# Two of four gate blocks with a second level of Winograd's scheme, in the last two groups of an attention and FFN kernel

## The chip, the cores and the metric

The kernel runs on one core of a Trainium2 chip. A core has five engines that run their own instruction streams and wait for each other by semaphores: TensorE (PE, matmuls out of SBUF into PSUM, with weight loads shown apart as PEld), VectorE (DVE), ScalarE (ACT), GpSimd (POOL) and SyncE (SP, which here only issues DMAs). The metric is the device time of one execution in microseconds, as the median of several runs.

## The reference

A linear attention whose normed output is the input of a multiplicative feed-forward network. All arrays are f32.

```python
batch, n_heads, seq, head_dim = (8, 8, 576, 64)
kv  = np.einsum('bhsd,bhse->bhde', k, v)
out = np.einsum('bhsd,bhde->bhse', q, kv)
rms = np.sqrt(np.mean(out * out, axis=-1, keepdims=True) + 1e-06)
attn_out = out / rms * g_norm
x = attn_out.transpose(0, 2, 1, 3).reshape(4608, 512)
# w1, w2: (512, 1024)   w3: (1024, 1024)   w_out: (1024, 512)
a = x @ w1
b = x @ w2
h = a * b @ w3
return h @ w_out
```

## The kernel before, in words

**Groups.** The 4608 tokens are worked in nine groups of 512: for each of the eight batches its first 512 tokens, and one group of the eight times 64 tokens that are left (called group 8, its input is `x_left`). The order is 0 to 6, then 8, then 7 (`groups`, L824). `w3 @ w_out` is folded into one matrix `w3o` at the start, so a group has two parts: the gates, ab = (x @ w1) * (x @ w2), and the output, ab @ w3o. The attention of the next batch is cut into pieces that are woven into the gates of the current group (`steps`, L518, called by `between`); groups 8 and 7 have none left to weave in.

**Winograd's scheme.** Every product of matrices is cut into 2 x 2 blocks and made with 7 block products in place of 8, with sums of blocks ahead (s1 to s4 of one side, t1 to t4 of the other) and behind. `winograd` (L610) is one such level: it keeps the products p1, p5, u2 and u3 by a ScalarE copy from PSUM (`keep`, L628), lets other products add up onto the same bank, and calls `done` for each of the four output blocks c12, c22, c11, c21, in that order.

**Gates.** `gates(T, p, between, ready)` (L742) makes a quarter of the gates of group T: p runs over the NF = 4 blocks. A product is 4 matmuls of 128 x 128 weights with 256 columns of x (two halves, for w1 and w2, and two chunks), so a block has 28. VectorE adds the two parts of an output block and multiplies its w1 half by its w2 half into `ab[i][:, p, j, :]` (L756, L757; for c21 L752, L753). Then `sum_ab(p)` makes the four sums of the block that the output needs (VectorE, 128x256). In the last block (p = 3) these sums, and the first of the inner ones, are given to `gates` as `ready` actions, and VectorE's order is from there on the written one (`in_order`, L1130). TensorE, GpSimd and SP are in the written order throughout; ScalarE is ordered by the scheduler.

**Output.** `project_twice(T, last, ahead)` (L864) uses two levels: 7 outer products of 7 inner products of 2 matmuls with 128 columns each, 98 matmuls. An outer product fills two PSUM banks, with 4 and 3 of its inner products (`products`, L877); `keep` (L908) copies both to SBUF on ScalarE, `add` (L937) adds a product from PSUM on VectorE, and `finish` (L914) makes an output block of the 7 inner products with four VectorE additions (L920 to L923). The inner sums of the ab side are made by `sum_inner` (L849) just ahead, into three sets of small tiles `inner_sums`, with the last one in place. The w3o side with all its sums is prepared once, in group 1 (`prepare_b`, L795), kept in DRAM (`w3o_l2`, 896 KB for each of the 7 parts), and streamed back for every group through three places in SBUF (`streams`) and the done group's x (`load_b`, L827; each load waits until the matmuls that read the place before are done). At the end of a group's output stage `load_b` has begun the first three parts of the next group's. `ahead` holds the four subtractions that make t1 to t4 of the next group's x (`combine_x`, L717).

**Pools.** `late_tile` gives the tiles p1, p5 and u (u2, u3 and u4 share one); PSUM has five banks named mm and three named at. `tick` (L542) is a one-column GpSimd copy whose only use is to wait for a late tile.

Of the kernel before, what the change touches and what calls it, by code (L numbers as in the profile page):

```python
# [2 lines left out]

# [8 lines left out]
FP32 = mybir.dt.float32  # L12
# [9 lines left out]
def kernel(  # L22
# [32 lines left out]
    nc = tc.nc  # L55
    PSUM = bass.MemoryType.PSUM
    P = 128

    B, H, S, D = q.shape
    DM = H * D  # L60
    DF = w1.shape[1]
    NP = H // 2
    KF = DF // P
    NH = KF // 2
    J = 4
    G = J * P
    N = G // 2
# [5 lines left out]
    inp = ctx.enter_context(tc.tile_pool(name="inp", bufs=2))  # L73
    work = ctx.enter_context(tc.tile_pool(name="work", bufs=2))
    ps_mm = ctx.enter_context(tc.tile_pool(name="ps_mm", bufs=5, space=PSUM))
    ps_at = ctx.enter_context(tc.tile_pool(name="ps_at", bufs=3, space=PSUM))
# [5 lines left out]
    def bank(pool, tag):  # L82
        return pool.tile([P, 512], FP32, name=tag, tag=tag)
# [31 lines left out]
    NF = KF // 2  # L115
# [488 lines left out]
    late = {}  # L604
    tick = const.tile([P, 1], FP32, name="tick")

    def late_tile(name):
        return late_pool.tile([P, 7, P], FP32, name=name[0] if name[0] == "u" else name)
# [65 lines left out]
    def run(*step_lists):  # L674

        for steps in zip(*step_lists):
            for step in steps:
                step()
# [38 lines left out]
    def combine_x(T):  # L717
        xb[T] = {f"b{i + 1}{j + 1}": xT[T][:, i, j] for i in range(2) for j in range(2)}
        return combine(xb[T], parts(xc))
# [9 lines left out]
    def sum_ab(p):  # L729
        aa[p] = {f"a{i + 1}{j + 1}": ab[j][:, p, i, :] for i in range(2) for j in range(2)}  # L730
        return sums(aa[p], free["ab", p])
# [10 lines left out]
    def gates(T, p, between, ready=lambda name: None):  # L742
        def done(name, one, two):
            multiply(name, one, two)
            ready(name)

        def multiply(name, one, two):

            dst = ab[int(name[1]) - 1][:, p, int(name[2]) - 1, :]
            if two is None:  # L750
                c = late_pool.tile([P, N], FP32, name="c21")
                nc.scalar.copy(c, one[:, 0, :])  # L752
                nc.vector.tensor_mul(dst, c, one[:, 1, :])  # L753
                return
            c = late_pool.tile([P, 2, N], FP32, name="c")
            nc.vector.tensor_add(c, one, two)  # L756
            nc.vector.tensor_mul(dst, c[:, 0, :], c[:, 1, :])  # L757

        winograd(
            lambda name, w, c: wa[p][name][:, w, c, :],  # L760
            lambda name, c: xb[T][name][:, c, :],
            NP // 2, done, between,
        )


    def project(T, between):
        def done(name, one, two):
            half, j = int(name[1]) - 1, int(name[2]) - 1
            dst = o_sbs[half][:, :, j * N:(j + 1) * N]
            if two is None:  # L770
                nc.scalar.copy(dst, one)
            else:
                nc.vector.tensor_add(dst, one, two)
            if name in ("c11", "c21"):
                rows = out[T * S:T * S + G, :].rearrange("(p j) f -> p j f", j=J)
                nc.sync.dma_start(out=rows[:, 2 * half:2 * half + 2, :], in_=o_sbs[half])

        winograd(
            lambda name, m, p: aa[p][name][:, m * P:(m + 1) * P],
            lambda name, p: ob[p][name],  # L780
            NF, done, between,
        )
# [12 lines left out]
    def prepare_b():  # L795

        nc.sync.dma_start(
            out=w3o_l2[7, :, 0:1024].rearrange("p (f n) -> p f n", n=N), in_=b_blocks()[5]
        )
        for n, y in enumerate(b_blocks()):  # L800
            b11, b12, b21, b22 = (
                y[:, 2 * i:2 * i + 2, j * P:(j + 1) * P] for i in range(2) for j in range(2)
            )


            stage = w3o_sums[0].rearrange("p f n -> p (f n)") if n == 4 else (
                o_sbs[(n - n // 5) % 2].rearrange("p m n -> p (m n)")
            )
            stage = stage[:, 0:6 * P]
            t1, t2, t4 = (t.rearrange("p (c n) -> p c n", n=P) for t in (  # L810
                stage[:, i * 2 * P:(i + 1) * 2 * P] for i in range(3)
            ))
            nc.vector.tensor_sub(t1, b12, b11)
            nc.vector.tensor_sub(t2, b22, t1)
            nc.vector.tensor_sub(b12, b22, b12)
            nc.vector.tensor_sub(t4, b21, t2)
            nc.sync.dma_start(
                out=w3o_l2[n, :, 0:1024].rearrange("p (f n) -> p f n", n=N), in_=y
            )
            nc.sync.dma_start(out=w3o_l2[n, :, 1024:PART], in_=stage)  # L820
            yield
# [5 lines left out]
    def load_b():  # L827
        n = len(loaded_b)
        if n == ALL_B:
            return  # L830
        i = n % 7
        t = streams[n % 3] if n < 7 else streams[(i + 1 if i < 3 else i) % 3]
        if n >= 7 and i == 3:
            done_with = xT[groups[1 + n // 7]]
            t = done_with.rearrange("p i j r n -> p (i j r n)")[:, 0:PART]

        part = {ALL_B - 2: 6, ALL_B - 1: 7}.get(n, n % 7)

        queue = nc.scalar if i in ((3, 5) if n < 7 else (4, 6)) else nc.sync
        if n + 1 < ALL_B:  # L840
            queue.dma_start(out=t, in_=w3o_l2[part])
        else:
            t = t[:, 0:1024]
            queue.dma_start(out=t, in_=w3o_l2[part, :, 0:1024])
        loaded_b.append(t)
# [15 lines left out]
        nc.vector.tensor_sub(a21, a11, a21)  # L861
        inner[n] = [a11, a12, a22, s1, s2, s4, a21]

    def project_twice(T, last, ahead):  # L864
        def store(half):
            if T < B:
                rows = out[T * S:T * S + G, :].rearrange("(p j) f -> p j f", j=J)
# [121 lines left out]

            add(p5, r1)  # L990
        z = keep("u3", r1)
        load_b()
        if not last:
            sum_inner(6)
            nc.vector.tensor_add(p5, p5, z)
        finish(p5, 1, 1)
        products(6 if last else 5, r2)
        load_b()
        if last:
            add(z, r2)  # L1000
            finish(z, 1, 0)
            last_block()
        else:
            add(p1, r2)
            finish(p1, 0, 0)
            products(6, r1)
            load_b()
            finish(keep("u4", r1), 1, 0)

    done = {}  # L1010
    dram = ctx.enter_context(tc.tile_pool(name="dram", bufs=1, space=bass.MemoryType.DRAM))
    w3o_l2 = dram.tile([8, P, PART], FP32, name="w3o_l2")


    ctx.enter_context(tc.manual_schedule(
# [92 lines left out]
    for n, T in enumerate(groups):  # L1108
        pieces = steps(T + 1) if n + 2 < NG else iter([])

        def between():
            next(pieces, lambda: None)()
            if T == 1:
                for _ in range(2):
                    if next(preparing, 0) == 0 and len(loaded_b) < 3:
                        load_b()

        for p in range(NF):
            if T and p + 1 == NF:
                sum_1, sum_2, sum_4, sum_3 = sum_ab(p)  # L1120
                following = {
                    "c12": [], "c22": [sum_1],
                    "c11": [
                        lambda: sum_inner(0, lambda: all_of(f() for f in (sum_2, sum_3))),
                        lambda: sum_inner(1),
                    ],
                    "c21": [sum_4],
                }

                in_order = tc.manual_schedule(engines={mybir.EngineType.DVE})  # L1130
                in_order.__enter__()
                gates(T, p, between, lambda name: all_of(f() for f in following[name]))
                continue
            gates(T, p, between if T or p else lambda: None)
            if T == 0:
                if p + 1 < NF:
                    run(sum_w(p + 1))
                for n in range(2):
                    if len(converted) < len(todo):
                        ahead = [copies["xT"] if p == 0 else copies["u3"][0], copies["u2"][p]][n]  # L1140
                        with tc.issue_after(ahead.ins):
                            begin_next()
                        end_next()
                if p + 1 == NF:
                    allocate_projection()
                    run(*(f(i) for i in range(NF) for f in (sum_ab, combine_w3o)))
            else:
                run(sum_ab(p))
        last = n + 1 == NG
        if T:  # L1150
            project_twice(T, last, [] if last else combine_x(groups[n + 1]))
            in_order.__exit__(None, None, None)
            continue
        project(T, between)
        run(combine_x(1))
        preparing = prepare_b()
        third = late_pool.tile([P, 3, 2, P], FP32, name="inner_sums")
        inner_sums.append([third[:, i] for i in range(3)])

# [29 lines left out]
```

## Time and profile before

| | us |
|---|---|
| median of 4 runs (767.14 to 769.38) | 767.76 |
| the profiled execution | 767.95 |
| its span | 766.2 |
| gates of group 8, four blocks (621.92 to 670.27 in the span) | 48.35 |
| output of group 8 (670.27 to 692.16) | 21.89 |
| gates of group 7, four blocks (692.16 to 740.51) | 48.35 |
| output of group 7 and the last stores (740.51 to 766.2) | 25.7 |

The span is the time between the first and the last instruction of the profiled execution; the 1.75 us that its time has more lie around it. Group 8 and group 7 have the same stages, one after the other. The granted TensorE clock is 1.00 in every stage listed.

How such lines are read: a timeline line has the start in us from the span's beginning, the length, the engine, the source line, the operation, what it writes and reads with the program's names (buffer numbers left out), shapes, a count when several alike are merged, and in brackets how long the engine stood idle before it and whose end released it. A line of a group table has, after the count, the busy time in us, the mean of one instruction in ns, and the idle time before. Program names in the trace are those of the place in SBUF: "raw" stands for the sums of ab and for the output tiles, "w3o_sb" for two of the three stream places.

### The profile page before, as it was taken

What the parts mean: (1) busy time and instruction counts of PE and PEld (TensorE: products, weight loads), DVE (VectorE), ACT (ScalarE), POOL (GpSimd) and SP (SyncE); (2) the same over time, 40 slices, a digit from 0 to 9 for tenths busy, and PEclk for the clock granted to TensorE, in tenths of its full rate; (3) what the DMA queues carried; (4) which work ended last, traced back from release to release, by engine and by line L of the source; (5) the groups of instructions that cost most, each with busy time, mean ns of one, the idle gap of its engine ahead of it and who ended that gap; (6) DMA issues with size and microseconds to landing.
All of it is one profiled execution on the core that took longest, in us unless ns stands there. A gap on an engine that the chain in (4) does not pass through costs nothing.

```text
span 766.2 us, 14419 instructions
## 1 busy us (share of the span) xinstructions
PE 758.0 (99%) x5775; PEld 659.4 (86%) x5775; DVE 543.3 (71%) x1083; ACT 253.2 (33%) x479; POOL 135.7 (18%) x132
## 2 busy tenths in 40 slices
PE   7999999999999999999999999999999999999998
PEld 5455788888899889988998899889988998898897
DVE  6977999548878468846775687667755864495467
ACT  6776764213222332233222322232133222222221
POOL 0000000223510441043114411331144000000000
PEclk9999999999999999999999999999999999999999
DMA  9997641338997836773568466835652560065024
GB/s 319 334 336 198 200 137 44 83 84 255 323 304 263 236 99 165 228 209 108 170 218 211 113 182 219 203 103 177 231 103 49 182 210 1 7 228 159 1 79 148
DMA packets 133159, 132.55 MB, mean 173 GB/s; under 512 B 76644, under 2 KB 121188, under 8 KB 133092
## 3 DMA queue, kind: packets, MB, share of 16 engines
q1 hardware_dynamic: 130640, 117.20, 52.3%
q10 hardware_dynamic: 2452, 14.42, 5.6%
q8 instruction: 46, 0.75, 0.4%
q14 instruction: 21, 0.17, 0.1%
HBM read 100.27 MB, written 16.38 MB: 152 GB/s over the span
## 4 chain that ended last, share of the span: by engine, by line
PE 97%; DMA 2%; ACT 0%; issue 0%; SPq 0%; DVE 0%; ACTq 0%
PE mm L617 60%; PE mm L899 23%; PE mm L596 7%; PE at L332 3%; PE at L415 2%; DMA raw<-in_moe_w_out_dram 1%; PE at L583 1%; PE at L351 1%; PE at L950 0%; DMA raw<-in_moe_w_dram 0%; PE at L449 0%; PE at L434 0%; ACT ab L157 0%; ACT kv_sb L343 0%; ACT chunks L158 0%; PE mm L434 0%
## 5 line engine op out<-in xcount | busy, mean ns | idle before, releaser
L617 PE MATMUL mm<-xT,w_sb 128*128 128x256 f32 x768 | 176.2, 379 | 0.0
L617 PEld LDWEIGHTS mm<-xT,w_sb 128*128 128x128 f32 x768 | 145.5, 190 | 20.0 <-issue 0.5
L617 PE MATMUL mm<-xc,ws 128*128 128x256 f32 x576 | 130.2, 379 | 0.0
L617 PEld LDWEIGHTS mm<-xc,ws 128*128 128x128 f32 x576 | 109.3, 190 | 15.0 <-ACT p L630 0.2
L756 DVE TENSOR_TENSOR c<-mm,u 128x512 f32<-128x512 f32 x36 | 24.9, 690 | 102.8 <-PE mm L617 102.8
L630 ACT COPY u<-mm 128x512 f32<-128x512 f32 x74 | 43.4, 587 | 137.8 <-PE mm L617 127.8
L630 ACT COPY p<-mm 128x512 f32<-128x512 f32 x74 | 43.4, 586 | 88.0 <-PE mm L617 84.7
L617 PE MATMUL mm<-xc,w_sb 128*128 128x256 f32 x288 | 69.0, 382 | 0.0
L596 PE MATMUL mm<-chunks,ab 128*128 128x512 f32 x128 | 60.3, 603 | 2.5 <-DVE chunks L170 1.7
L290 POOL COPY xT<-xn 128x1024 uint16<-128x1024 uint16 x26 | 31.2, 1227 | 177.7 <-DVE xn L393 177.7
L617 PE MATMUL mm<-xT,ws 128*128 128x256 f32 x256 | 61.1, 381 | 0.0
L617 PEld LDWEIGHTS mm<-xc,w_sb 128*128 128x128 f32 x288 | 53.9, 190 | 7.7 <-ACT u L630 0.3
L757 DVE TENSOR_TENSOR ab<-c 128x256 f32<-128x256 f32 x108 | 57.9, 536 | 3.0
L617 PEld LDWEIGHTS mm<-xT,ws 128*128 128x128 f32 x256 | 48.0, 190 | 6.6
L384 DVE TENSOR_REDUCE inv<-sq 128x8 f32<-128x512 f32 (+1 forms) x40 | 23.4, 627 | 39.3 <-ACT sq L383 39.3
L899 PE MATMUL mm<-w3o_sb,raw 128*128 128x128 f32 x372 | 48.6, 276 | 0.1
L899 PE MATMUL mm<-w3o_sb,ab 128*128 128x128 f32 x368 | 48.6, 275 | 0.0
L756 DVE TENSOR_TENSOR c<-p,u 128x512 f32<-128x512 f32 x36 | 27.1, 752 | 27.4 <-ACT u L630 27.4
L899 PEld LDWEIGHTS mm<-w3o_sb,ab 128*128 128x128 f32 x368 | 45.4, 192 | 0.4
L899 PEld LDWEIGHTS mm<-w3o_sb,raw 128*128 128x128 f32 x372 | 44.9, 192 | 0.5 <-DVE raw L857 0.2
L596 PEld LDWEIGHTS mm<-chunks,ab 128*128 128x128 f32 x128 | 21.8, 190 | 25.1 <-issue 15.8
L910 ACT COPY u<-mm 128x512 f32<-128x512 f32 x23 | 13.5, 586 | 85.7 <-DVE raw L923 63.3
(166 smaller groups left out, 1169.0 us busy)
## 6 DMA issues: line engine op xcount, KB each, us to landing
w3o_sb<-w3o_l SPq DMA_DIRECT2D x18, 896.0 KB, 6.1
raw<-in_moe_w_dram SPq DMA_DIRECT2D x31, 512.0 KB, 7.4
raw<-w3o_l SPq DMA_DIRECT2D x15, 896.0 KB, 4.7
w3o_sb<-w3o_l ACTq DMA_DIRECT2D x14, 896.0 KB, 4.5
k_sb<-in_k_dram SPq DMA_DIRECT2D x32, 256.0 KB, 3.8
v_sb<-in_v_dram SPq DMA_DIRECT2D x32, 256.0 KB, 4.7
q_sb<-in_q_dram SPq DMA_DIRECT2D x32, 256.0 KB, 4.2
out_dram<-raw SPq DMA_DIRECT2D x14, 512.0 KB, 3.5
```

The source lines that it names most:

```text
L290: nc.gpsimd.tensor_copy(to, src.rearrange("p a n w -> p w a n"))
L332: nc.tensor.matmul(kv_ps[e * D:(e + 1) * D, r - rs[0], :], lhsT=k_sb[:, e, cols] if j < J else kl[:, 2 * r + e, :], rhs=v_sb[:, e, cols] i ...
L351: nc.tensor.transpose(qt_ps[:, e, i, :], q_sb[:, e, i * P:(i + 1) * P], ident)
L384: nc.vector.tensor_reduce(out=inv[:, i], in_=sq.rearrange("p (h d) -> p h d", d=D), axis=AX.X, op=ALU.add)
L415: nc.tensor.matmul(o_ps[l][tokens, n * D:(n + 1) * D], lhsT=qT[r][rows, e, i, tokens], rhs=kv_b[rows, e, r, :], start=True, stop=True,)
L596: nc.tensor.matmul(sums_ps[half][m], lhsT=w3T[half, c][:, m, :], rhs=chunks[:, c, 1, :], start=(c == 0), stop=(c == KF - 1),)
L617: nc.tensor.matmul(ps[:, u, :], lhsT=lhsT(a_name, u, c), rhs=rhs(b_name, c),  start=(u == 0 and c == 0 and to is None), stop=(c == chunks ...
L630: copies.setdefault(name, []).append(nc.scalar.copy(t, ps))
L756: nc.vector.tensor_add(c, one, two)
L757: nc.vector.tensor_mul(dst, c[:, 0, :], c[:, 1, :])
L899: nc.tensor.matmul(to[:, i, :], lhsT=x[:, c, :], rhs=y[:, c, :], start=new and place // 4 not in seen, stop=(c == 1), skip_group_check=True,)
L910: nc.scalar.copy(t[:, 0:4], ps[0])
```

## The change

In groups 8 and 7 (`TWICE`) the gates are made in the order: block 2 as before, then blocks 0 and 1 together with a second level, then block 3 as before.

- `gates_of_two(T)` runs the 7 outer products in two column halves (w = 0 for w1, w = 1 for w2). Each outer product is again cut in 2 x 2: the weights by the two blocks (m) and the two chunks (c), x by its two chunks and the two halves of its 256 tokens. So an outer product is 7 matmuls of 128 columns in two PSUM banks, 49 for a half and 98 for the two halves. The order of the outer products is written so that the output block c11 comes first (after two products); its second product goes to two of the at banks. Product 5 and product 6 of a half both go to the banks of `r1`. The copies of u3 and u4 go to places of their own (`places`, in the tile names xT and xn), the rest to p1, p5 and u as before. Each half makes its four output blocks with `finish`; the second half writes to a tile c and multiplies it into the first half's result.
- The inner sums of the weights (s1, s2, s4 of each of the 7 outer blocks, 128x256 each) are made once on VectorE in groups 3 and 4 by `prepare_w`, one of its seven steps in each call of `between` in blocks 0 and 1, and stored to DRAM (`w_l2`) from SP. The fourth sum is made in place in group 6, block 2 (`replace_a21`). They come back in three loads of 896 KB (`load_w`), issued at the end of the output stage ahead of group 8 and of group 7 where `load_b` was called; the three `load_b` calls stand in `gates_of_two` instead, in its second half.
- The inner sums of x (4 for each of the 7 outer blocks, 28 of 128x128) are made by GpSimd in block 2 (`sum_x`), behind a `tick` on p1, into the places of k, v, q and qT tiles, which have no other use by then.
- The four sums of ab for blocks 0 and 1 are made by GpSimd with four instructions for both blocks (`sum_ab_two`), behind `gates_of_two`, in place of `sum_ab(0)` and `sum_ab(1)` on VectorE.
- VectorE's written order begins at `gates_of_two` in these groups.

```diff
+    def w_blocks(name):
+        return [wa[m][name][:, :, c, :] for m in range(2) for c in range(2)]
+
+    def prepare_w():
+        for n, (name, _) in enumerate(PRODUCTS):
+            a11, a12, a21, a22 = w_blocks(name)
+            s1, s2, s4 = inner_sums[2 * (n % 2)]
+            nc.vector.tensor_add(s1, a21, a22)
+            nc.vector.tensor_sub(s2, s1, a11)
+            nc.vector.tensor_sub(s4, a12, s2)
+            for i, s in enumerate((s1, s2, s4)):
+                at = (3 * n + i) * 2 * P
+                nc.sync.dma_start(
+                    out=w_l2[:, at:at + 2 * P].rearrange("p (w m) -> p w m", w=2), in_=s
+                )
+            yield
+
+    def replace_a21():
+        for name, _ in PRODUCTS:
+            a11, _, a21, _ = w_blocks(name)
+            nc.vector.tensor_sub(a21, a11, a21)
...
+    def load_w():
+        n = len(loaded_w)
+        t = streams[(n + 1) % len(streams)]
+        nc.sync.dma_start(out=t, in_=w_l2[:, n * PART:(n + 1) * PART])
+        loaded_w.append(t)
...
+    def sum_x(T):
...
+        nc.gpsimd.tensor_copy(tick, late["p1"][:, 0, 0:1])
+        for t, (_, name) in zip(x_sums, PRODUCTS):
+            b11, b12, b21, b22 = (
+                xb[T][name][:, c, i * P:(i + 1) * P] for c in range(2) for i in range(2)
+            )
+            t1, t2, t3, t4 = t
+            nc.gpsimd.tensor_sub(t1, b12, b11)
+            nc.gpsimd.tensor_sub(t2, b22, t1)
+            nc.gpsimd.tensor_sub(t3, b22, b12)
+            nc.gpsimd.tensor_sub(t4, b21, t2)
...
+    def gates_of_two(T):
...
+        def products(n, w, ps, new):
...
+            for place, x, y in (
+                (0, a11, b11), (3, a12, b21), (1, a22, t4), (2, s1, t1), (6, s2, t2), (5, s4, b22),
+                (4, s3, t3),
+            ):
+                nc.tensor.matmul(
+                    ps[place // 4][:, place % 4, :], lhsT=x, rhs=y,
+                    start=new and place // 4 not in seen, stop=True, skip_group_check=True,
+                )
+                seen.add(place // 4)
+            if w == 1 and n in (2, 4, 6):
+                load_b()
+            return ps
...
+        def finish(z, w, i, j):
...
+            dst = ab[i][:, 0:2, j, :].rearrange("p m (n t) -> p m n t", t=P)
+            to = dst
+            if w:
+                to = late_pool.tile([P, 2, N], FP32, name="c").rearrange("p m (n t) -> p m n t", t=P)
+            nc.vector.tensor_add(z[:, 6], z[:, 6], z[:, 0])
+            nc.vector.tensor_add(z[:, 4:6], z[:, 4:6], wide(6))
+            nc.vector.tensor_add(to[:, 1], z[:, 1:3], wide(4))
+            nc.vector.tensor_add(to[:, 0], z[:, 3:6:2], z[:, 0:3:2])
+            if w:
+                nc.vector.tensor_mul(dst, dst, to)
+
+        for w in range(2):
+            r1 = products(0, w, banks(ps_mm, "mm"), True)
+            p1 = keep(late_tile("p1"), r1)
+            r3 = products(1, w, banks(ps_at, "at"), True)
+            add(p1, r3)
+            finish(p1, w, 0, 0)
+            r2 = products(2, w, banks(ps_mm, "mm"), True)
+            p5 = keep(places[2] if w else late_tile("p5"), r2)
+            products(3, w, r1, False)
+            z = keep(late_tile("u2"), r1)
+            products(4, w, r2, False)
+            add(z, r2)
+            finish(z, w, 0, 1)
+            products(5, w, r1, False)
+            u3 = keep(places[0], r1)
+            nc.vector.tensor_add(p5, p5, u3)
+            finish(p5, w, 1, 1)
+            products(6, w, r1, False)
+            finish(keep(places[1], r1), w, 1, 0)
+        loaded_w.clear()
+
+    def sum_ab_two():
+        c11, c12, c21, c22 = (ab[i][:, 0:2, j, :] for i in range(2) for j in range(2))
+        s1, s2, s4 = (t[:, 0:2] for t in ab_sums)
+        nc.gpsimd.tensor_add(s1, c12, c22)
+        nc.gpsimd.tensor_sub(s2, s1, c11)
+        nc.gpsimd.tensor_sub(c12, c11, c12)
+        nc.gpsimd.tensor_sub(s4, c21, s2)
...
+    PRODUCTS = [
+        ("a11", "b11"), ("a12", "b21"), ("s1", "t1"), ("s2", "t2"), ("s4", "b22"), ("s3", "t3"),
+        ("a22", "t4"),
+    ]
+    TWICE = (B, B - 1)
...
+            if T in (3, 4) and p < 2:
+                next(preparing_w, 0)
+            if T == B - 2 and p == 2 and not replaced:
+                replaced.append(True)
+                replace_a21()
+
+        if T in TWICE:
+            once = iter([T])
+            gates(T, 2, lambda: [sum_x(t) for t in islice(once, 1)])
+            run(sum_ab(2))
+            in_order = tc.manual_schedule(engines={mybir.EngineType.DVE})
+            in_order.__enter__()
+            gates_of_two(T)
+            sum_ab_two()
         for p in range(NF):
+            if T in TWICE and p + 1 < NF:
+                continue
...
-            project_twice(T, last, [] if last else combine_x(groups[n + 1]))
+            project_twice(
+                T, last, [] if last else combine_x(groups[n + 1]),
+                load_w if not last and groups[n + 1] in TWICE else load_b,
+            )
```

In `project_twice` the three `load_b()` calls behind products 4, 5 and 6 become `load_after()`, its new argument.

## The prediction

> **What bounds the kernel.** I read the engine totals and the chain that ended last first, then the timeline of TensorE over the last two groups, then tables by stage of that stretch, and last the timelines of VectorE, ScalarE and GpSimd there.
>
> ```profile
> PE 758.0 (99%) x5775; PEld 659.4 (86%) x5775; DVE 543.3 (71%) x1083; ACT 253.2 (33%) x479; POOL 135.7 (18%) x132
> PE 97%; DMA 2%; ACT 0%; issue 0%; SPq 0%; DVE 0%; ACTq 0%
> ```
>
> TensorE is busy 99% and holds 97% of the chain: only fewer or cheaper matmuls, or new gaps between them, can move the time. The stage table of group 8 (columns: stretch, its length, busy us and instructions of PE, PEld, DVE, ACT, POOL, granted clock, DMA share, GB/s), four gate blocks and the output stage:
>
> ```profile
> 621.92:634.01 12.09, 12.09 (x58) 10.65 (x57) 6.46 (x15) 2.82 (x5) 0.00 (x0) 1.00 0.59 193
> 634.01:646.10 12.09, 12.09 (x57) 10.64 (x56) 5.21 (x12) 2.72 (x5) 0.00 (x0) 1.00 0.00 0
> 646.10:658.19 12.09, 12.09 (x58) 10.64 (x57) 5.21 (x12) 2.72 (x5) 0.00 (x0) 1.00 0.00 1
> 658.19:670.27 12.08, 12.08 (x57) 10.64 (x56) 5.20 (x12) 2.72 (x5) 0.00 (x0) 1.00 0.06 8
> 670.27:692.16 21.89, 21.89 (x198) 21.88 (x196) 20.82 (x51) 5.12 (x10) 0.00 (x0) 1.00 0.67 229
> ```
>
> A gate block is 7 products x 4 matmuls of 256 columns, in the trace 56 instructions (an f32 matmul is two): 12.09/56 = 0.2159 us each, with no gap. The output stage is 98 matmuls of 128 columns, 196 instructions: 21.89/196 = 0.1117. Two narrow ones cost 0.2234, 3.5% more than one wide one: part of what the second level saves is lost to this. In the gate blocks VectorE is 43% busy, GpSimd idle and DMA nearly idle.
>
> **Matmuls removed.** Blocks 0 and 1 of groups 8 and 7 (2 x 56 wide instructions, 24.18 us a group) become 2 column halves x 7 products x 7 matmuls of 128 columns, 196 instructions, as many as the output stage: 196 x 0.1117 = 21.89. Gain 2.29 a group, **4.58 for both**. That is the ceiling.
>
> **A new wait on TensorE.** Products 5 and 6 of each half go one after the other into the same two banks, and between them ScalarE must copy the first result out. Nothing of the sort stands in the old stages, where another product always lies between. Its price comes from these rows:
>
> ```profile
> 602.02 0.59 ACT L910 COPY p<-mm 128x512 f32<-128x512 f32 x1 [1.41 <-PE mm L899]
> 603.37 0.48 ACT L911 COPY p<-mm 128x384 f32<-128x384 f32 x1 [0.75 <-PE mm L899]
> ...
> 70.28 0.61 ACT L588 COPY ab<-at 128x512 f32<-128x512 f32 x1
> ...
> 70.95 0.30 PEld L596 LDWEIGHTS mm<-chunks,ab 128*128 128x128 f32 x2 [0.82 <-ACT ab L588]
> ```
>
> The product that the first copy reads began at 600.04 and had issued its 16 instructions for that bank at 601.83; the copy started 0.19 later and took 0.59. At 70.95 a weight load followed the copy's end (70.89) by 0.06. A product of 14 instructions lasts 1.56, its first bank is complete after 8 (0.89). So the copy ends at 0.89 + 0.19 + 0.59 = 1.67, the next load goes at 1.73, and without the wait it would have gone at 1.56 less the 0.1 to 0.15 that loads run ahead: a gap of 0.17 (if only the matmul waits) to 0.32. The second bank's copy ends at 2.25, before the product gets there. I take 0.30, nearest to the row where the load waited: four such places, **1.2** (0.7 to 1.3).
>
> **GpSimd's sums of x.** Per group 28 subtractions of 128x128 f32 replace nothing on VectorE; they are new. They wait for the copy of p1 in block 2 (about 2.4 us into it) and are first needed at its end (12.09), the last four by product 6 of the first half: 12.09 + 6 x 1.56 + 0.45 = 21.9. So 28 have 19.5 us, **0.70 each**. The trace has no subtraction on GpSimd. Nearest rows:
>
> ```profile
> L304 POOL COPY x_left<-xn_left 128x512 uint16<-128x512 uint16 x8 | 5.1, 661 | 0.0
> masks.py:199 POOL TENSOR_SCALAR_AFFINE_SELECT ident<-ident 128x128 f32<-128x128 f32 x1 | 0.3, 292 | 0.1
> ```
>
> One input of the same shape takes 0.29; four times as many (16-bit) elements take 0.66. Between these I take 0.41: copies of 1024 and 512 elements (1.15 and 0.66) give about 1 ns an element and 0.15 fixed, and two inputs read 256. 28 x 0.41 = 11.5 us, ready about 14 against the first need at 12.5 (four of them) and the last at 21.9: cost **0**. At 0.66 it is 18.5, just inside; above 0.70 TensorE waits.
>
> The Trainium skill ("GPSIMD Engine Reference", section 4.1 Engine selection) speaks against this: two-input elementwise work belongs on VectorE, GpSimd being about half as fast. Its measured 4497 ns for 2048 elements, scaled to 128, is an estimate of 0.28 us before any fixed cost; by it, too, the sum stays as it is, so the rule costs nothing here unless the cover of 19.5 us goes.
>
> **VectorE in the two blocks.** Its work doubles. Prices from the output stage before:
>
> ```profile
> 618.11 1.08 DVE L995 TENSOR_TENSOR p<-p,u 128x896 f32<-128x896 f32 x1
> 619.23 0.29 DVE L920 TENSOR_TENSOR p<-p 128x128 f32<-128x128 f32 x1
> ...
> 620.69 0.69 DVE L938 TENSOR_TENSOR p<-mm,p 128x512 f32<-128x512 f32 x1
> ...
> 621.88 0.29 DVE L920 TENSOR_TENSOR p<-p 128x128 f32<-128x128 f32 x1
> ...
> 623.34 0.28 DVE L920 TENSOR_TENSOR u<-u 128x128 f32<-128x128 f32 x1
> ```
>
> From start to start: p5 plus u3 1.12, an add of a product 1.19 (620.69 to 621.88), a finish of four instructions 1.46 (to 623.34). A half has two adds, one p5, four finishes: 9.34; the second half has four multiplies of 512 columns besides, at 0.80 (0.69 and a dependent start): 12.54. Sum 21.88 against TensorE's 21.89 + 0.6. Laid out in order, add p1 can begin 3.2 after the blocks' start, the first half is done at 14.6, the second at 28.0, that is 5.5 to 5.8 into block 3. There c12's add starts 7.19 into the block (629.11 - 621.92) and VectorE then idles 1.12 before c22: it may come free as late as 8.3. Cover 2.5 us, cost **0**. TensorE never waits for VectorE inside the blocks: the banks it reuses are freed by ScalarE's copies, or by adds more than 4 us earlier; nor do the copies, since u3 and u4 of the halves have tiles of their own and the others were finished with 5 us before.
>
> What can eat the cover is GpSimd beside it:
>
> ```profile
> 586.70 1.49 POOL L292 COPY qT_left<-xn_left 128x1024 uint16<-128x1024 uint16 x1
> ...
> 587.33 1.14 DVE L757 TENSOR_TENSOR ab<-c 128x256 f32<-128x256 f32 x1
> ```
>
> The multiply, 0.42 alone, took 1.14 beside a copy; the longest of 108 took 1.25. So an overlap costs VectorE 0.36 (0.78 at 569.79) to 0.83. The four sums of ab (512 columns, at 1 ns per input element about 1.2 us each) start when c22 is ready, 25.8, and end about 31: four overlaps, at most 3.3 against 2.5 of cover, so 0 to 0.8 a group. I take **0**: four at the middle of the two, 0.6, are 2.4. Their readers, the sums inside the output stage, come at 34: 3 us of room.
>
> The skill's page "SBUF — State Buffer" (section Who interferes with whom) says that a VectorE instruction with two SBUF inputs and a GpSimd one that reads SBUF exclude each other, the second waiting in full. The rows agree (0.72 longer beside a 1.49 copy). By the rule at its worst the loss would be four times 1.2 less the cover, 2.3 a group.
>
> **The rest.** Weight sums in groups 3 and 4: 7 calls of three subtractions and adds of 0.42 (0.34 to 0.45 a start), 1.2 us a call, in gate blocks where VectorE idles 4.2 us in a row (before 327.22 and 341.92); uncovered, 8.6 in all. Their 21 stores of 128 KB stand in SP's queue ahead of k, v and q loads that are fetched two pairs ahead; a 128 KB store takes 2.9 us to land: 0, up to 1 if a load comes late. Replacing a21 in group 6: 7 x 0.42 = 2.9 in block 2, where VectorE idles 5.49 before 581.09. Loads: three of 896 KB a group, plus the usual three moved into the second half. Such loads land in 4.5 to 6.1 us; the last of the weights is issued at the output stage's end and read 18 us later, the last moved one at the end of the two blocks and read by product 2 of the output stage, 12.09 + 3.1 later, as DMA idles. SP holds only loads of the same chain behind them. The four sums of blocks 0 and 1 leave VectorE (8 x 0.34 a group): no gain, TensorE did not wait for them.
>
> **Sum.** 4.58 - 1.2 = 3.4. Against the profiled execution (767.95, its span 766.2 and 1.75 around it): 764.55; that run lies 0.19 above the median, so **764.4**. Its own bounds: 763.2 (no gap) to 766.1 (gaps 1.3, VectorE 2 x 0.8).
>
> **Rivals.**
> 1. *GpSimd's x sums are late* (the slower side). Against: 0.41 by the rows, GpSimd otherwise empty. For: no such instruction in the trace, VectorE runs beside it. From 0.76 a sum the gain is gone (28 x 0.06 x 2 = 3.4); at 0.90 TensorE waits 5.6 a group: 764.4 + 11.2 = 775.6. Chance 0.13.
> 2. *VectorE is the bound*: ten overlaps a group at 0.36 take 3.6, 1.1 over the cover, and the output stage starts late twice: 766.6. For: 21.88 against 21.89. Against: 2.5 of cover. Chance 0.17.
> 3. *No gap at all*, the copies being faster than I count: 763.2. Chance 0.08.
>
> **How the numbers follow.** The forecast has 0.62. A measurement of this kernel tells changes above about 0.2% (1.5 us) from none, so faster ends at 766.2: the forecast and the third rival, 0.70, a third of the second, 0.06, and 0.01 of the first: 0.77. Same: 0.10 of the second and 0.02 of the first, 0.12. Slower: 0.11, nearly all GpSimd. The range runs from 763.2, below which only unseen gains lie, to 766.9, which leaves out a little of the second rival and the first.
>
> **What would show it.** Right: the two blocks take 21.9 plus two gaps of about 0.3 between products 5 and 6, put down to ScalarE's copy; GpSimd's subtractions last 0.3 to 0.5 and end within 4 us of the blocks' start; VectorE's last multiply ends 5 to 7 us into block 3; the old output stages and groups 3, 4, 6 keep their lengths. Wrong: TensorE's gaps inside the first half released by GpSimd; a gap at the output stage's first sums released by VectorE; subtractions above 0.70.

## The result, and the profile after

| | before | changed |
|---|---|---|
| median, us | 767.74 (61 runs) | 766.80 (40 runs) |
| ratio of the two | 1 | 0.9989, 95% interval 0.9983 to 0.9994 |
| the profiled execution and its span | 767.95, 766.2 | 766.71, 764.9 |

The kernel became 0.9 us faster, 0.11%, where 3.4 were forecast: less than the 1.5 us that the prediction asked of a change before it calls it faster. The engine totals and the chain after:

```profile
PE 757.1 (99%) x5943; PEld 662.2 (87%) x5943; DVE 588.2 (77%) x1159; ACT 263.2 (34%) x499; POOL 175.0 (23%) x198
PE 81%; issue 6%; DVE 5%; DMA 5%; POOL 2%; ACT 1%; SPq 1%; DVEq 0%; POOLq 0%; ACTq 0%
```

TensorE is still busy 99%, but has lost 16 points of the chain: it is now released by others at some places. Busy time does not show this (in the output stage below TensorE counts 22.29 busy for the instructions that took 21.89 before), so the stages were measured by the starts of their first matmuls. Group 8 by stage, block 2, the two blocks together, block 3, output (columns as before):

```profile
623.01:635.10 12.09, 12.09 (x59) 10.64 (x57) 6.75 (x14) 2.82 (x5) 9.12 (x20) 1.00 0.60 197
635.10:657.53 22.43, 22.42 (x198) 22.04 (x197) 19.25 (x42) 10.38 (x20) 4.74 (x10) 1.00 0.23 77
657.53:669.62 12.09, 12.09 (x59) 10.64 (x58) 11.51 (x17) 2.97 (x6) 5.27 (x4) 1.00 0.29 92
669.62:692.02 22.40, 22.29 (x197) 22.02 (x196) 21.30 (x52) 5.12 (x10) 0.00 (x0) 1.00 0.68 226
```

The two blocks took 22.43 in place of 24.18, the output stage 22.40 in place of 21.89, and VectorE is busy 11.51 of 12.09 in block 3, where it was 5.20. Group 8 also starts at 623.01 in place of 621.92: 1.1 us had been lost before the new matmuls ran. The same starts for every kernel that ran, in us (gates of groups 3 and 4; two blocks, block 3 and output of group 8; then the time at which group 2 starts; a1 to g2 are the experiments below):

```
kernel    gates 3  gates 4  two blocks  block 3  output   group 2 at   span
before     53.56    54.38     24.18      12.08    21.89    243.78     766.2
changed    53.69    55.59     22.43      12.09    22.40    243.52     764.9
a1         54.33    55.15     22.42      12.09    22.41    243.12     764.7
b1         53.69    55.61     22.43      12.09    21.88    244.28     764.6
b2         53.68    55.61     22.43      12.09    22.07    242.98     763.7
c1         53.69    55.60     22.15      12.09    22.43    244.10     765.0
d1         53.56    54.38     22.43      12.09    22.42    242.78     762.8
e1         53.69    55.59     22.64      13.99    21.88    242.84     767.4
f1         53.56    54.38     22.16      12.09    21.88    243.68     762.1
e2         53.55    54.38     22.64      13.81    21.89    244.16     767.0
g1         53.69    55.62     22.43      12.09    22.43    243.04     764.5
g2         53.55    54.38     22.16      12.09    21.88    242.87     761.3
```

Every stage listed repeats to about 0.03 us between kernels that share its code. What runs ahead of group 2 does not: its end moves by 1.5 us, and by 0.5 and 0.8 between two runs of the same kernel (changed and g1, f1 and g2). Of this, the output of group 1 alone takes between 22.28 (g2) and 23.61 (g1). So the stages say what an edit does; a single span carries the part before group 2 with it.

The sum of the profiled execution, by stages: gates of groups 8 and 7 each 48.35 to 46.61, 3.48 gained; output of group 8 0.51 and of group 7, with the end, 0.63 lost (25.66 to 26.29); groups 3 and 4 0.13 and 1.21 lost; what runs ahead of group 2 0.26 gained. Together 1.26 gained; the two spans, 766.17 and 764.92, differ by 1.25.

The weight loads' waits from 300 us on show who releases TensorE now (columns: who waits for whom, us in total, times, longest):

```profile
PEld mm L618 <- ACT p L631: 1.8, 3, 1.2
PEld mm L850 <- ACT xT L863: 0.8, 4, 0.2
PEld mm L1049 <- DVE ab L1011: 0.6, 2, 0.3
```

The second line is the predicted gap, four times. The first and third are not in the sum of the prediction.

**Where 1.2 us went in group 4.** The timeline of the changed kernel there, all engines:

```profile
408.10 2.21 POOL L293 COPY qT<-q_sb 128x1024 uint16<-128x1024 uint16 x2 [6.07 <-PE at L416]
...
408.67 0.75 DVE L775 TENSOR_TENSOR raw<-w_sb 128x256 f32<-128x256 f32 x1 [1.06 <-DMA w_l<-raw]
409.34 1.25 DVE L672 TENSOR_TENSOR raw<-raw,ab 128x256 f32<-128x256 f32 x1
...
412.48 1.27 DVE L385 TENSOR_REDUCE inv<-sq 128x8 f32<-128x512 f32 x2
...
413.79 0.31 ACT L389 ACTIVATE inv<-inv,eps_col 128x16 f32<-128x16 f32 x1 [3.04 <-DVE inv L385]
...
414.00 1.05 ACT L631 COPY p<-mm 128x512 f32<-128x512 f32 x2
...
414.62 1.38 PEld L618 LDWEIGHTS mm<-xc,ws 128*128 128x128 f32 x7 [1.22 <-ACT p L631]
```

Before the change, VectorE idled 0.70 ahead of the norm's reduction:

```profile
409.11 1.28 DVE L384 TENSOR_REDUCE inv<-sq 128x8 f32<-128x512 f32 x2 [0.70 <-ACT sq L383]
```

L775 is the first of the three new weight sums. It waits 1.06 for the store of an earlier sum from the same place; L672, two old sums of ab queued behind it (409.34 and 410.52), then run beside GpSimd's copies at 1.25 each in place of 0.42. So the reduction (L385) comes at 412.48 in place of 409.11. ScalarE stands 3.04 us at the norm's square root, the copy of p1 is queued behind that, and TensorE waits 1.22 for the copy. The other 0.13 of group 4, and the 0.13 of group 3, are lost at the group's start, where a weight load waits 0.27 for a copy of p1 (398.83 and 323.27; the experiment a1 shows why). In group 3 new sums stood ahead of the norm too (333.22) and its reduction came 2.0 later, but no load waited there.

**Where 0.5 us went in each output stage.** The changed kernel at the end of the two blocks of group 8:

```profile
660.72 1.27 POOL L911 TENSOR_TENSOR raw<-ab,ab 128x512 f32<-128x512 f32 x1 [20.72 <-DVE ab L885]
662.06 1.33 POOL L912 TENSOR_TENSOR raw<-raw,ab 128x512 f32<-128x512 f32 x1
...
660.81 1.46 DVE L881 TENSOR_TENSOR xT<-xT 128x256 f32<-128x256 f32 x1
662.30 1.38 DVE L882 TENSOR_TENSOR c<-xT 128x256 f32<-128x256 f32 x1
663.60 1.48 DVE L883 TENSOR_TENSOR c<-xT 128x256 f32<-128x256 f32 x1
...
665.94 0.69 DVE L757 TENSOR_TENSOR c<-mm,u 128x512 f32<-128x512 f32 x1
666.67 0.83 DVE L758 TENSOR_TENSOR ab<-c 128x256 f32<-128x256 f32 x1
667.61 0.69 DVE L757 TENSOR_TENSOR c<-p,u 128x512 f32<-128x512 f32 x1
...
672.72 0.52 PEld L1049 LDWEIGHTS mm<-w3o_sb,ab 128*128 128x128 f32 x4 [0.30 <-DVE ab L1011]
```

Before the change, block 3 of group 8 began at 658.19 and had idle time ahead of c12's and of c22's addition:

```profile
665.37 0.69 DVE L756 TENSOR_TENSOR c<-mm,u 128x512 f32<-128x512 f32 x1 [5.56 <-PE mm L617]
...
667.64 0.69 DVE L756 TENSOR_TENSOR c<-p,u 128x512 f32<-128x512 f32 x1 [1.12 <-ACT u L630]
```

GpSimd's sums of ab begin as VectorE makes its last output block. Three additions of 0.42 take 1.46, 1.38 and 1.48: VectorE is 3.06 later. c12's addition (665.94) starts 8.41 into block 3 where 7.18 was usual, and c22's (667.61) 10.08 into it where 9.45 was usual, 0.6 later. From there VectorE has no idle time until the inner sums of the output, and TensorE waits for one of them (L1011).

### The profile page after: what moved, and what is told of

It is laid out like the page before. It is cut to its first block, busy times and chain, and to the rows that moved or that the text cites. A ratio compares the mean times of both kernels' runs of the same rounds, so it can differ in the third digit from the quotient of the medians.

```text
span 764.9 us, 15018 instructions
## 1 busy us (share of the span) xinstructions
PE 757.1 (99%) x5943; PEld 662.2 (87%) x5943; DVE 588.2 (77%) x1159; ACT 263.2 (34%) x499; POOL 175.0 (23%) x198
## 4 chain that ended last, share of the span: by engine, by line
PE 81%; issue 6%; DVE 5%; DMA 5%; POOL 2%; ACT 1%; SPq 1%; DVEq 0%; POOLq 0%; ACTq 0%
PE mm L618 44%; PE mm L1049 18%; PE mm L597 7%; PE mm L850 4%; PE at L333 2%; PE at L416 2%; DMA raw<-in_moe_w_out_dram 1%; DMA w3o_sb<-w3o_l 1%; PE at L850 1%; DMA w_l<-raw 1%; PE at L584 1%; DMA xn<-xT 1%; DMA q_sb<-qT 1%; POOL xT L305 1%; DVE c L882 1%
## 5 line engine op out<-in xcount | busy, mean ns | idle before, releaser
L618 PE MATMUL mm<-xT,w_sb 128*128 128x256 f32 x720 | 165.2, 379 | 0.0
L618 PEld LDWEIGHTS mm<-xT,w_sb 128*128 128x128 f32 x720 | 136.3, 190 | 18.7 <-issue 0.5
L618 PE MATMUL mm<-xc,ws 128*128 128x256 f32 x512 | 116.3, 380 | 0.8 <-ACT p L631 0.8
L618 PEld LDWEIGHTS mm<-xc,ws 128*128 128x128 f32 x512 | 97.0, 190 | 14.9 <-ACT p L631 1.8
L631 ACT COPY u<-mm 128x512 f32<-128x512 f32 x66 | 38.7, 586 | 123.6 <-PE mm L618 108.3
L291 POOL COPY xT<-xn 128x1024 uint16<-128x1024 uint16 x26 | 31.4, 1235 | 177.3 <-DVE xn L394 177.3
L631 ACT COPY p<-mm 128x512 f32<-128x512 f32 x66 | 38.5, 584 | 73.7 <-PE mm L618 66.5
L618 PE MATMUL mm<-xc,w_sb 128*128 128x256 f32 x256 | 61.4, 383 | 0.0
L618 PE MATMUL mm<-xT,ws 128*128 128x256 f32 x240 | 57.3, 382 | 0.0
L618 PEld LDWEIGHTS mm<-xc,w_sb 128*128 128x128 f32 x256 | 47.8, 190 | 6.9 <-ACT u L631 0.3
L385 DVE TENSOR_REDUCE inv<-sq 128x8 f32<-128x512 f32 (+1 forms) x40 | 23.4, 627 | 35.8 <-ACT sq L384 35.8
L1060 ACT COPY u<-mm 128x512 f32<-128x512 f32 x23 | 13.5, 585 | 86.9 <-DVE raw L1073 57.5
L305 POOL COPY xT<-xn 128x1024 uint16<-128x1024 uint16 x26 | 30.6, 1206 | 53.0 <-DMA xn<-xT 53.0
```

The source lines that it names most:

```text
L291: nc.gpsimd.tensor_copy(to, src.rearrange("p a n w -> p w a n"))
L305: nc.gpsimd.tensor_copy(words(dst), src)
L385: nc.vector.tensor_reduce(out=inv[:, i], in_=sq.rearrange("p (h d) -> p h d", d=D), axis=AX.X, op=ALU.add)
L618: nc.tensor.matmul(ps[:, u, :], lhsT=lhsT(a_name, u, c), rhs=rhs(b_name, c),  start=(u == 0 and c == 0 and to is None), stop=(c == chunks ...
L631: copies.setdefault(name, []).append(nc.scalar.copy(t, ps))
```

## The experiments

Each kernel is the changed one with the edit shown. Ratios are to the kernel before, run on the same chip.

### Three places for the weight sums (a1)

```diff
-            s1, s2, s4 = inner_sums[2 * (n % 2)]
+            s1, s2, s4 = inner_sums[n % 3]
```

> The weight sums of groups 3 and 4 use three sets of places in turn in place of two, so that a sum no longer waits for the store of the sum two steps before; nothing else changes. Theory (the store's return holds VectorE, the norm of the attention comes 3.4 us late, ScalarE stands at the square root with the copy of p1 behind it, and TensorE waits 1.22 at 414.62): the gates of group 4 go from 55.59 back to 54.4 to 54.7, no weight load of group 4 waits longer than 0.3, the span falls by 0.9 to 1.2 and the median to about 765.7. Rival (it is GpSimd's copies beside the sums, 1.25 in place of 0.42, that make the norm late, whenever the sums run there): the gates of group 4 stay above 55.2 and the time at 766.5 to 767.

Measured: 767.41 us, ratio 0.9998 (0.9988 to 1.0007). The wait for the store was gone, group 4 fell to 55.15 only, and group 3 rose to 54.33: 1.54 above before in the two, against 1.34. Neither the theory nor its rival was put to the test, for VectorE's order was another one: the three sums of group 4 now all stood among the output's additions, and none in the norm. How much of the 3.4 us in the norm is the store's and how much GpSimd's stays open. VectorE's timeline, ScalarE's and TensorE's at the start of group 3:

```profile
320.49 0.42 DVE L775 TENSOR_TENSOR raw<-w_sb 128x256 f32<-128x256 f32 x1
320.82 0.28 DVE L1070 TENSOR_TENSOR p<-p 128x128 f32<-128x128 f32 x1
321.02 0.42 DVE L776 TENSOR_TENSOR raw<-raw,w_sb 128x256 f32<-128x256 f32 x1
...
322.37 0.42 DVE L1073 TENSOR_TENSOR raw<-p 128x256 f32<-128x256 f32 x1
...
322.87 1.07 ACT L631 COPY p<-mm 128x512 f32<-128x512 f32 x2 [2.80 <-DVE raw L1073]
...
323.51 1.59 PEld L618 LDWEIGHTS mm<-xc,ws 128*128 128x128 f32 x8 [0.90 <-ACT p L631]
```

The weight sums, written into the gates of group 3, stand in VectorE's order among the additions of the output of group 2 (L1070 to L1073). These are the last readers of the tile p1, ScalarE's next copy into it waits for them 2.80 us, and TensorE 0.90. In the changed kernel two of the calls stand there too (316.97 and 320.25 for group 3, 392.54 and 395.82 for group 4), at a wait of 0.27 for TensorE, and a third in the norm (333.22 and 408.67); group 3's fourth, at 342.40, held no weight load. VectorE is ordered by the scheduler up to the last gate block, so where the program calls a sum does not say where it runs. That gave the next theory, tried in d1.

### The sums of ab on VectorE (b1)

`sum_ab_two` with `nc.vector` in place of `nc.gpsimd`.

> The four sums of ab for blocks 0 and 1 go to VectorE in groups 8 and 7, behind the second level's last block, as four instructions of 512 columns. Theory (the output stages of groups 8 and 7 start 0.5 late each because GpSimd's sums hold VectorE's last finish, 3 instructions at 1.4 in place of 0.42): VectorE saves these 3.1 us and pays 4 x 0.65 = 2.6, and the longer multiply (0.83 for 0.42) is gone too; the output stage of group 8 goes from 22.40 to 21.9 to 22.1, that of group 7 alike, the median falls by 0.6 to 1.0. Rival (VectorE has simply too much to do in the two blocks, whoever makes the sums): the output stages stay at 22.3 to 22.6, the median at 766.8.

Measured: 765.50 us, ratio 0.9972 (0.9964 to 0.9981); output of group 8 21.88, all of the 0.51 back. In VectorE's timeline the last additions are at 0.42 again and the four sums follow:

```profile
662.40 0.42 DVE L883 TENSOR_TENSOR c<-xT 128x256 f32<-128x256 f32 x1
662.85 0.69 DVE L885 TENSOR_TENSOR ab<-ab,c 128x512 f32<-128x512 f32 x1
663.46 0.68 DVE L911 TENSOR_TENSOR raw<-ab,ab 128x512 f32<-128x512 f32 x1
...
665.99 0.68 DVE L757 TENSOR_TENSOR c<-mm,u 128x512 f32<-128x512 f32 x1
666.71 0.42 DVE L758 TENSOR_TENSOR ab<-c 128x256 f32<-128x256 f32 x1
```

The first of the four starts at 663.46, the addition behind them at 665.99, so VectorE pays 2.53 for the sums where it had paid 3.06 for GpSimd making them. The rival, that VectorE has too much to do whoever makes them, falls: c22's addition comes 9.46 into block 3 again. GpSimd saved VectorE nothing here.

### The sums of ab in halves (b2)

Eight instructions of 256 columns on GpSimd, block by block, in place of four of 512.

```diff
+        for _, c12, _, c22, s1, _, _ in blocks:
+            nc.gpsimd.tensor_add(s1, c12, c22)
+        for c11, _, _, _, s1, s2, _ in blocks:
+            nc.gpsimd.tensor_sub(s2, s1, c11)
...
```

> GpSimd still makes the four sums of ab, as eight instructions of 256 columns in place of four of 512. Theory (a VectorE instruction with both inputs in SBUF waits until the GpSimd instruction that runs has ended): VectorE's three additions beside them take 0.7 to 0.85 each in place of 1.4, VectorE is through 1.7 us earlier than in the changed kernel (at or before 7.2 into block 3), and the output stages of groups 8 and 7 take 21.9 to 22.0: 0.9 to 1.1 less in all. Rival (the two share a path, and what counts is the amount of GpSimd's work): the additions' excess sums up to 3 us again, and the output stages stay at 22.3 or more.

Measured: 765.75 us, ratio 0.9980 (0.9971 to 0.9989); output of group 8 22.07.

```profile
660.18 1.59 POOL L914 TENSOR_TENSOR raw<-ab,ab 128x256 f32<-128x256 f32 x2 [20.43 <-DVE ab L885]
...
660.27 0.91 DVE L881 TENSOR_TENSOR xT<-xT 128x256 f32<-128x256 f32 x1
661.22 0.83 DVE L882 TENSOR_TENSOR c<-xT 128x256 f32<-128x256 f32 x1
661.98 0.94 DVE L883 TENSOR_TENSOR c<-xT 128x256 f32<-128x256 f32 x1
662.96 1.10 DVE L885 TENSOR_TENSOR ab<-ab,c 128x512 f32<-128x512 f32 x1
```

The three additions' excess is 0.49, 0.41 and 0.52, half of what it was, with GpSimd's instruction half as wide (0.73 to 0.91 in place of 1.27 to 1.44) and as many elements in all. In the changed kernel each of the three ended 0.28 or 0.29 after the GpSimd instruction beside it, and here 0.27 or 0.28 after. That is what waiting for the instruction that runs gives, and not the sharing of a path. Three more instructions now fall among them: the multiply (1.10 for 0.69), one behind c12 (0.69 for 0.42) and c22's addition (0.98 for 0.69), so the excess is still 2.4 in all, against 3.5. 0.19 of the loss stays.

### Another product between products 5 and 6 (c1)

```diff
+            if not w:
+                begun_r1.append(products(0, 1, banks(ps_at, "at"), True))
             products(6, w, r1, False)
```

The second half takes its r1 from there and its r3 from the mm banks.

> Product 0 of the second half goes between products 5 and 6 of the first half, into two at banks; the sums made are the same. Theory (TensorE waits there for ScalarE's copy of r1 and for nothing else): of the four waits of 0.17 to 0.3 the two of the first halves are gone, the two blocks of a group take 22.1 to 22.2 in place of 22.43, the span falls by 0.5. Rival (the gap between products has another cause, such as the bank being started anew): the two blocks stay at 22.4, the span unchanged.

Measured: 766.11 us, ratio 0.9978 (0.9970 to 0.9987). The two blocks fell to 22.15 in both groups, 0.28 each, and two of the four waits for the copy of u3 are gone: the gap is the copy. In the changed kernel products take 1.56 from start to start, but product 5 takes 1.73 and product 6 1.67, in both halves; here the first half's take 1.56. The span did not fall (765.0), because group 2 began at 244.10 in that execution, 0.58 later than in the changed kernel's. The place as it was in the changed kernel:

```profile
644.01 0.59 ACT L863 COPY xT<-mm 128x512 f32<-128x512 f32 x1 [1.98 <-PE mm L850]
...
644.64 0.52 PEld L850 LDWEIGHTS mm<-xc,w_sb 128*128 128x128 f32 x4 [0.20 <-ACT xT L863]
```

The copy ends at 644.60 and the load follows after 0.04. Why product 6 loses 0.11 besides stays open.

### The weight sums placed (d1)

One call a block, in blocks 0 to 2 of groups 3 to 5, each held behind a named VectorE instruction (`latest` keeps the output stage's last addition and the last multiply of a gate block).

```diff
-            if T in (3, 4) and p < 2:
-                next(preparing_w, 0)
+            between_calls.append((T, p))
+            if T in (3, 4, 5) and p < 3 and between_calls.count((T, p)) == 1:
+                with tc.issue_after(latest["output" if p == 0 else "gates"].ins):
+                    next(preparing_w, 0)
```

> The weight sums are made once a block, in the first call of blocks 0, 1 and 2 of groups 3, 4 and 5, and each is held behind a named VectorE instruction (the output stage's last addition, or the last multiply of the block before), so that it falls into the 4 to 6 us in which VectorE idled. Theory (the sums cost time by where they stand in VectorE's order: ahead of the last output block's additions they hold the tile p1 and ScalarE's copy into it, in the norm they hold ScalarE's square root): gates of groups 3, 4, 5 at 53.56, 54.38, 53.56 as before the change, 1.34 less than in the changed kernel; no weight load waits for the copy of p1; span about 763.6, median about 765.5. Rival (the 21 stores or the extra DMA traffic hold the attention's loads): the gates of groups 3 to 5 stay 1 us or more above those of before.

Measured: 765.24 us, ratio 0.9968 (0.9954 to 0.9981). Groups 3 and 4 are back at 53.56 and 54.38, and no load waits for p1. The sums stand behind the output's last addition, and the norm comes with 0.69 of idle time ahead of it, as before the change:

```profile
397.01 0.42 DVE L1074 TENSOR_TENSOR raw<-u 128x256 f32<-128x256 f32 x1
397.35 0.42 DVE L776 TENSOR_TENSOR inner_sums<-ws 128x256 f32<-128x256 f32 x1
...
408.10 1.28 DVE L385 TENSOR_REDUCE inv<-sq 128x8 f32<-128x512 f32 x2 [0.69 <-ACT sq L384]
```

The same 21 instructions and 21 stores cost nothing there: their place was the cost, not their work and not the DMA.

### c11 late (e1)

Product 1, the addition of it and c11's `finish` move between products 5 and 6, in both halves; the three `load_b` calls move with the places that they overwrite.

> The early output block is undone alone: product 1 stands between products 5 and 6 in both halves, and c11 is made there. Theory (the wait for ScalarE's copy is the price of c11 first): the two blocks of a group take 21.9 in place of 22.43, with no weight load waiting for the copy of u3; VectorE, without c11's early work, ends later, and the output stages go from 22.40 to between 22.4 and 23.4: together within 0.8 of the changed kernel either way. Rival (c11 first costs and brings nothing): blocks 22.4 and output stages 22.4 as they are.

Measured: 770.20 us, ratio 1.0029 (1.0015 to 1.0043). A miss in size and place: the output stage was not late at all (21.88), but block 3 took 13.99 and the two blocks 22.64. ScalarE's and TensorE's lines in block 3:

```profile
661.67 0.58 ACT L631 COPY p<-mm 128x512 f32<-128x512 f32 x1 [0.37 <-DVE c L883]
...
662.31 1.59 PEld L618 LDWEIGHTS mm<-xc,ws 128*128 128x128 f32 x8 [2.03 <-ACT p L631]
```

c11 late keeps the tile p1 in use until VectorE is through with it (L883), block 3's first copy goes into that tile, and TensorE waits 2.03 for it. In the two blocks the second half's p1 waits in the same way (0.68 in each group). Block 3, the two blocks and the output stage together take 58.51 in place of 56.92, so c11 first wins 1.6 us a group over c11 late although it pays 0.54 for its gap.

### Three edits together, and c11 late with two of them (f1, e2)

f1 is d1, b1 and c1 in one kernel.

> Three edits together: the weight sums placed once a block, the sums of ab on VectorE, product 0 of the second half between products 5 and 6 of the first. If each cost is its own: 1.34 + 1.03 + 0.56 less than the changed kernel, span about 762.0, median 763.9, ratio to before 0.995. If they share their cause (VectorE too full at the end), the output stages show it: above 22.1, and the median above 764.5.

Measured: 763.78 us, ratio 0.9940 (0.9920 to 0.9961), span 762.1; the stages are those of the single edits. Each cost is its own.

e2 is d1 and b1 with c11 late.

> The weight sums placed once a block, the sums of ab on VectorE, and c11 late. If VectorE's end decides: its end comes 1 to 2 us later than with c11 first, the sums of ab behind it, and the output stages start 0.5 to 2 late, so slower than the kernel with product 0 between (763.9) by 0.5 to 3 us. If VectorE has room: blocks 21.9 with no gap, output stages 21.9, span about 761.5, median 763.3, the best of all.

Measured: 768.53 us, ratio 1.0005 (0.9992 to 1.0017), 4.8 us above f1. As in e1 the loss is in block 3 (13.81), not in the output stage where the expectation put it; GpSimd makes no sums of ab here, so they are not its cause.

### Changed and mended side by side (g1, g2)

> The changed kernel once more, beside the mended one on the same chip. Its stages should repeat to 0.05 us (gates of group 4 at 55.6, two blocks at 22.43, output stage of group 8 at 22.4), with only group 1 moving by some tenths; ratio to before 0.9983 to 0.9994.

Measured: 766.58 us, ratio 0.9986 (0.9977 to 0.9995).

> The kernel with the three edits once more: stages as in its first run (53.56 and 54.38 in groups 3 and 4, two blocks at 22.16, output stages at 21.88), 2.9 us below the changed kernel, ratio to before 0.994 to 0.996. If the first run's gain was the chip's and not the edits', the two come closer than 2 us.

Measured: 763.47 us, ratio 0.9950 (0.9938 to 0.9963): 3.1 us below the changed kernel on the same chip, and 4.1 below the kernel before. Every run of the one (762.89 to 764.29) lies below every run of the other (765.90 to 767.72).

## Why the prediction was wrong

**Matmuls removed: right.** 24.18 less the measured 22.43 is 1.75 a group. The products without a gap took 1.56 from start to start; 14 of them at the pace of the old output stage are 21.89, the predicted number, and the gaps make the rest, 0.54.

**The gap between products 5 and 6: right.** 1.2 was taken, 0.54 a group or 1.1 measured, with loads waiting 0.20 each; c1, where one gap of a group's two goes away with the wait and takes 0.28 with it, shows that the copy is the cause.

**GpSimd's sums of x: right.** 0.41 was taken. The changed kernel has 0.45 each where VectorE does not hold them (0.90 at most), and the 28 take 14.0 us in place of 11.5:

```profile
625.96 0.45 POOL L817 TENSOR_TENSOR k_sb<-x_left 128x128 f32<-128x128 f32 x1
626.49 0.46 POOL L818 TENSOR_TENSOR k_sb<-x_left,k_sb 128x128 f32<-128x128 f32 x1
...
639.50 0.50 POOL L820 TENSOR_TENSOR qT<-xc,qT 128x128 f32<-128x128 f32 x1
```

The last ends at 640.0, 4.9 into the two blocks where within 4 was forecast, and no load waits for GpSimd: the cover reached to 9.8. VectorE lost time beside them (0.56 to 0.67 in place of 0.42 around 636), which its idle time took up. The Trainium skill ("GPSIMD Engine Reference", section 4.1 Engine selection) spoke against them, and VectorE is indeed the faster one, by 1.6 rather than by 2: it takes 0.29 for that shape. Off the path it does not matter.

**VectorE in the two blocks and GpSimd beside it: the price failed.** "I take 0: four at the middle of the two, 0.6, are 2.4" against a cover of 2.5. The overlaps cost 1.04, 0.96, 1.06 and 0.41, together 3.5, since GpSimd's 512-column sums last 1.27 to 1.44, three of VectorE's four came just behind their starts, and each ended 0.28 or 0.29 after the sum beside it; in the prediction's row the multiply (587.33) began 0.63 into the copy of 1.49 and so caught only the rest of it. What the cover did not take comes out as 0.6 at c22 and 0.5 in the output stage, 1.1 in both groups. So the second rival's mechanism happened, at half its price, and b1 and b2 show it. The plan of VectorE's own work held: in b1, without GpSimd beside it, its last multiply of the two blocks ended 5.2 into block 3, where 5 to 7 was forecast, and in the changed kernel 8.3. The skill's page "SBUF — State Buffer" (section Who interferes with whom) gives the mechanism, and these rows agree with it. The worst case that the prediction worked out by it, 2.3 a group over the cover, was too high by about as much as the 0 taken was too low: it was 1.0 (3.5 less 2.5).

**The weight sums in groups 3 and 4: the step that failed most.** It said "1.2 us a call, in gate blocks where VectorE idles 4.2 us in a row" and took 0. Measured: 1.34. The cover existed, and d1 uses it; but the sums did not stand in it. The working took the place of the call in the program for the place in VectorE's order, which the scheduler makes in these groups: two calls of each group ran among the last output additions of the group before, and the third ahead of the attention's norm. It named VectorE's idle time and not what stood behind the sums: the readers of p1, and with the norm ScalarE's square root with p1's next copy behind it. In group 3 the place ahead of the norm cost nothing, in group 4 1.08.

Of the forecast's 3.4 us, 1.34 were lost to the weight sums and 1.1 to VectorE beside GpSimd, both of which the sum held at 0, and the gaps gave 0.1 back; that leaves 1.1, against 0.9 measured by the medians and 1.3 by the spans. The difference between these is smaller than what the part before group 2 moves by.

**Left open.** The gap of the second half (0.27 a group) was not removed, and what moves the part before group 2 from run to run is known in part alone: in five of the six runs in which the output of group 1 took 23.0 us or more, TensorE waited 0.20 to 0.75 there for a part of w3o to land from DRAM, and in the runs below that it did not.

## What to carry to other kernels

Work that is "hidden in idle time" has to be looked up in the order in which its engine runs it, not where the program calls it: if a scheduler orders that engine, name the instruction that it is to follow, and list who waits for the instructions behind it. A sum moved off a full engine to another one is not free if the two exclude each other: in the last microseconds of a stage it cost VectorE more (3.06) than making it itself (2.53). An overlap is priced by what is left of the other engine's instruction, up to the whole of it, and not by the middle of a few rows. Finishing a tile early can be worth more than the gap that the reordering opens, when the next stage's first copy goes into that tile.

## What the hardware showed that was not expected

VectorE's wait beside GpSimd has the grain of GpSimd's instruction (0.96 to 1.06 beside one of 1.27 to 1.44, 0.41 to 0.52 beside one of 0.73 to 0.91; each held addition ended 0.27 to 0.29 after it), and only instructions with both inputs in SBUF showed it: c12's addition, with one input in PSUM, kept its 0.69 at 665.94 while GpSimd's last sum ran from 665.95, and in b2 at 664.19 beside a sum that ran from 663.47.
